# Sign folded into the exponent by a parametric ReLU when float64 gate, value and out weights are converted

## The chip, the cores and the metric

The program runs on 1 core of one Trainium2 chip. The metric is device time in microseconds (us) for one execution. In the names of the trace PE is TensorE (PEld its weight loads), DVE is VectorE, ACT is ScalarE, POOL is GpSimd and SP is SyncE, whose queue (SPq) issues the transfers here.

## The reference

Attention with a local window and block summaries feeds a gated feed-forward layer with an RMS norm, and that feeds a second feed-forward layer with an ELU.

```python
def _moe_ref(x, w_gate, w_val, w_out, rms_g):      # x: 1536 x 512, d_ff 1536
    rms = np.sqrt(np.mean(x * x, axis=-1, keepdims=True) + 1e-06)
    xn = x / rms * rms_g
    g = xn @ w_gate
    silu = g * (1.0 / (1.0 + np.exp(-g)))
    val = xn @ w_val
    return (silu * val @ w_out).astype(np.float32)

def _moe2_ref(x, w_in, w_out):                     # d_ff 2048
    h = x @ w_in
    g = np.where(h > 0.0, h, np.exp(np.minimum(h, 0.0)) - 1.0)
    return (g @ w_out).astype(np.float32)
```

The attention has 2 batches, 8 heads, 768 positions and a head size of 64. The five weight matrices arrive as float64, so the kernel has to turn them into float32 itself.

## The kernel before

The 1536 tokens are three blocks of 512. Attention runs in 24 tiles of 64 positions (`add_tile`): scores `s`, row maximum `nm`, exponentials `e`, the transposed weights `at`, their copy `ats`, and the product with the values, `pv`, which is copied into `xT`. Block 0 is normed in two halves of 256 tokens (`add_norm`): squares `sq`, their sums by matmul `pss`, the mean on VectorE (`ms`), the inverse root on GpSimd (`y`), diagonals `dg` on VectorE, and the matmul `prs` that spreads them over the partitions, after which `scale_x` scales `xT`. A wide name such as `ss0slice(256, 512, None)` is the second half of `pss0`, `rs0slice(256, 512, None)` the second half of `prs0`.

Each block then goes through 12 chunks of the first layer (`add_block1`: gate `pg`, value `pv_0c` to `pv_11c`, product `th` and `act`, down projection `acc`) and later through 16 chunks of the second (`add_block2`: `ph`, `ex`, `act`, `acc`). Matmul operands are split into a high part (a cast on ScalarE, line 272) and a low part (a subtraction, line 283), and three products of the parts are summed. Chunk 0 of block 0 skips the split and multiplies in plain float32 (`project_f32`, line 836).

A weight tile is 128 x 512 numbers. `fetch` (lines 376 and 379) loads it as float64 into `st_<kind><chunk>`, where the kinds are g, v, o (gate, value, out) and i, p (the second layer). There are four `st` buffers, and `fetch` of a fifth tile waits until one is free. Four steps convert a tile:

- `convert_a` (line 278, ScalarE) scales the high 32-bit words, read as float32, by 2^-112, in place, which moves the exponent to the bias of float32;
- `convert_b` (line 395, VectorE) shifts them left by three bits and masks the sign away, into `raw_<kind><chunk>`;
- `convert_c` (line 400, VectorE) puts the sign bit back;
- `convert_d` (line 406, VectorE) adds the bits that the low words hold, and with it the `st` buffer is free.

The order on every engine and on SyncE's queue comes from a planner, `Order.issue`. Each step is added with an engine or a choice of them, a cost and a due time; the planner runs a list schedule with those costs, takes the ready step with the earliest due time on each engine, and then issues the steps in the order in which they started. Engines work through that order strictly. A table `SHIFT` moves the due times of some steps by stage (the names `convert_b`, `convert_c` and `convert_d` are among its keys). VectorE and GpSimd are taken to share a port, so the planner lets the steps named in `SHARED` run on one of them at a time.

Of the kernel before, what the change touches and what calls it, by code (L numbers as in the profile page):

```python
# [16 lines left out]
AF = mybir.ActivationFunctionType  # L17
ALU = mybir.AluOpType
# [19 lines left out]
class Order:  # L38
# [15 lines left out]
    def add(self, engine, cost, due, fn, *args, r=(), w=(), new=()):  # L54

        due += SHIFT.get((fn.__name__, sum(due >= x for x in EDGES)), 0)
        self.ops.append((engine, cost, due, fn, args, tuple(r), tuple(w), tuple(new)))
# [133 lines left out]
def fused_kernel(ctx: ExitStack, tc: tile.TileContext, q, k, v, w_gate, w_val, w_out, rms_g, w_in2, w_out2, out):  # L191
    nc = tc.nc
# [19 lines left out]
    scale = 1.0 / math.sqrt(D)  # L212
# [3 lines left out]
    add = o.add  # L216
    PE, ACT, DVE, POOL = "PE", "ACT", "DVE", "POOL"
# [8 lines left out]
    def new(tag, name, shape, dtype=F32):  # L226
        T[name] = pools[tag].tile(shape, dtype, tag=tag, name=name)
        return T[name]
# [47 lines left out]
    def times(eng, out, in_, factor):  # L276
        if eng == ACT:
            nc.scalar.mul(out, in_, factor)
        else:
            nc.vector.tensor_scalar_mul(out, in_, factor)  # L280
# [45 lines left out]
    for var in range(3):  # L326
# [11 lines left out]
        out=bb, in_=bb, pattern=[[-half, 8]], compare_op=ALU.is_ge, fill=0.0, base=0, channel_multiplier=1)  # L338
    nc.gpsimd.affine_select(
        out=bb, in_=bb, pattern=[[half, 8]], compare_op=ALU.is_ge, fill=0.0, base=half - 1, channel_multiplier=-1)  # L340
# [14 lines left out]
    for i in range(B * NQ):  # L355
        blk, r = divmod(i, TPB)
# [7 lines left out]
    for c in range(C1):  # L364
        t = chunk1_at[0, c]
        weights += [("g", c, t), ("v", c, t + 2.6), ("o", c, t + 5.2)]
    for c in range(C2):

        t = chunk1_at[NBLK - 1, 0] + 10 + 5.2 * c
# [13 lines left out]
    def words(kind, c):  # L383
        return T[f"st_{kind}{c}"].bitcast(U32).rearrange("p (n w) -> p n w", w=2)[:, :, 1]
# [2 lines left out]

    def convert_a(eng, kind, c):
        hi = words(kind, c).bitcast(F32)
        times(eng, hi, hi, 2.0 ** -112)  # L390

    def convert_b(kind, c):
        hi = words(kind, c)
        t = new("raw", f"raw_{kind}{c}", [P, 512], U32)
        nc.vector.tensor_scalar(
            t, hi, 3, 0x7FFFFFF8, op0=ALU.logical_shift_left, op1=ALU.bitwise_and)

    def convert_c(kind, c):
        t = T[f"raw_{kind}{c}"]
# [8 lines left out]
    def add_weights(kind, c, need):  # L408
        st, raw = f"st_{kind}{c}", f"raw_{kind}{c}"
        add("SP", 1.46, need - (14 if need > T0 + 20 else LEAD), fetch, kind, c, w=[st], new=[("st", st)])  # L410
        add(ANY_SB, 0, need - 8, convert_a, kind, c, r=[st], w=[st])
        add(DVE, 0.34, need - 7, convert_b, kind, c, r=[st], w=[raw], new=[("raw", raw)])
        add(DVE, 0.6, need - 6.5, convert_c, kind, c, r=[st, raw], w=[raw])
        add(DVE, 0.6, need - 6, convert_d, kind, c, r=[st, raw], w=[raw])

    def split_a(eng, b, kind, c):
# [559 lines left out]
    for i in range(B * NQ):  # L976
        b, t = divmod(i, NQ)
# [3 lines left out]
        blk, r = divmod(i, TPB)  # L981
# [7 lines left out]
    for kind, c, need in weights:  # L989
        add_weights(kind, c, need)  # L990
# [5 lines left out]

LOOK, URGENT = 0.2, 20
A0, A_GAP, LATER = 12.1, 1.275, -1.0  # L1000
PRE_0, PRE, VS0, MEAN = 0, 8, 4.5, 9.0
# [56 lines left out]
```

## Time and profile before

| | |
|---|---|
| median of 3 runs | 654.74 us (654.32 to 657.03) |
| profiled execution: time | 653.92 us |
| profiled execution: span of the instructions | 652.2 us |
| TensorE matmul busy | 639.4 us, 98% |
| VectorE busy | 477.2 us, 73% |
| ScalarE busy | 374.5 us, 57% |
| GpSimd busy | 68.7 us, 11% |

The profiled execution took 653.92 us, of which 652.2 us are the span from its first instruction to its last; the other 1.7 us lie around it. The profiled execution is 0.8 us under the median of the runs shown. A busy TensorE is one with a matmul in its pipeline: matmuls overlap, so one that is recorded with 389 ns can start 227 ns after the one before it.

### The profile page before, as it was taken

How to read it: one execution, taken by the hardware profiler on the slowest of the kernel's cores; microseconds unless marked ns; L12 is line 12 of the kernel's file. 1: busy time of each engine (PE TensorE's matmuls, PEld its weight loads, DVE VectorE, ACT ScalarE, POOL GpSimd, SP SyncE). 2: the span in 40 equal slices, each digit the busy share in tenths (PEclk: the TensorE clock that was granted, in tenths of full speed). 3: DMA queues.
4: the chain of work that ended last, by engine and by line, in shares of the span. 5: the costliest groups of instructions: out<-in, count | busy, mean ns of one | idle time of the engine just before them, and what ended most of it. 6: DMA issues, size and time to landing. Idle time of an engine off the chain costs nothing.

```text
span 652.2 us, 9445 instructions
## 1 busy us (share of the span) xinstructions
PE 639.4 (98%) x3440; PEld 528.4 (81%) x3440; DVE 477.2 (73%) x860; ACT 374.5 (57%) x829; POOL 68.7 (11%) x125
## 2 busy tenths in 40 slices
PE   7899999999999999999999999999999999999997
PEld 5788787888888888888888888888888888888886
DVE  6899998998945545599999996555675555755554
ACT  5887888878856655655555555443454444544441
POOL 4731103125200100300000000000000000000000
PEclk9999999999999999999999999999999999999999
DMA  9785995653120400003655520000010000100001
GB/s 255 196 236 163 268 282 162 200 168 88 33 47 3 140 1 2 0 13 119 205 180 163 162 65 1 0 1 1 1 65 0 2 0 1 53 13 2 0 1 64
DMA packets 69917, 54.70 MB, mean 84 GB/s; under 512 B 29168, under 2 KB 64176, under 8 KB 69872
## 3 DMA queue, kind: packets, MB, share of 16 engines
q1 hardware_dynamic: 69872, 54.11, 28.8%
q8 instruction: 27, 0.44, 0.3%
q14 instruction: 18, 0.15, 0.1%
HBM read 49.68 MB, written 3.15 MB: 81 GB/s over the span
## 4 chain that ended last, share of the span: by engine, by line
PE 91%; DVE 3%; DMA 2%; ACT 2%; SPq 1%; issue 1%; POOL 0%; ACTq 0%; POOLq 0%
PE acc L893 35%; PE ph L825 20%; PE pg L825 14%; PE s L617 3%; PE pv L667 2%; PE pv_7c L825 1%; PE pv_9c L825 1%; PE pv_11c L825 1%; PE pv_1c L825 1%; DMA va<-vs 1%; PE pv_10c L825 1%; PE pv_6c L825 1%; PE pv_5c L825 1%; PE pv_8c L825 1%; PE pv_2c L825 1%; PE pv_3c L825 1%
## 5 line engine op out<-in xcount | busy, mean ns | idle before, releaser
L825 PE MATMUL ph<-xb,ws_i 128*128 128x512 f32 x576 | 137.9, 389 | 0.0
L893 PE MATMUL acc<-ws_p,act 128*128 128x512 f32 x576 | 137.7, 389 | 0.0
L825 PEld LDWEIGHTS ph<-xb,ws_i 128*128 128x128 f32 x576 | 108.1, 188 | 22.5
L893 PEld LDWEIGHTS acc<-ws_p,act 128*128 128x128 f32 x576 | 108.1, 188 | 22.4
L893 PE MATMUL acc<-act,ws_o 128*128 128x512 f32 x432 | 106.4, 393 | 0.0
L825 PE MATMUL pg<-x,ws_g 128*128 128x512 f32 (+1 forms) x432 | 106.3, 390 | 0.0
L893 PEld LDWEIGHTS acc<-act,ws_o 128*128 128x128 f32 x432 | 80.2, 188 | 16.6
L825 PEld LDWEIGHTS pg<-x,ws_g 128*128 128x128 f32 x432 | 78.2, 188 | 15.3 <-issue 0.2
L283 DVE TENSOR_TENSOR ws_p<-raw_p,ws_p 128x512 fp32r<-128x512 f32 x48 | 33.1, 690 | 48.8 <-ACT ws_p L272 48.8
L272 ACT CAST ws_p<-raw_p 128x512 fp32r<-128x512 f32 x48 | 29.8, 621 | 63.1 <-PE ph L825 57.3
L272 ACT CAST act<-ex 128x512 fp32r<-128x512 f32 x48 | 29.8, 622 | 55.9 <-DVE ex L873 39.3
L880 DVE TENSOR_TENSOR act<-ex,act 128x512 fp32r<-128x512 f32 x48 | 33.1, 691 | 31.3 <-ACT act L272 30.9
L283 DVE TENSOR_TENSOR ws_i<-raw_i,ws_i 128x512 fp32r<-128x512 f32 x48 | 33.1, 689 | 19.1 <-ACT ws_i L272 19.0
L272 ACT CAST ws_i<-raw_i 128x512 fp32r<-128x512 f32 x48 | 29.7, 619 | 28.5 <-PE ph L825 23.1
L283 DVE TENSOR_TENSOR ws_g<-raw_g,ws_g 128x512 fp32r<-128x512 f32 x35 | 25.6, 732 | 18.4 <-ACT ws_g L272 18.0
L272 ACT CAST ws_o<-raw_o 128x512 fp32r<-128x512 f32 x36 | 22.4, 621 | 26.3 <-PE acc L893 6.3
L272 ACT CAST ws_g<-raw_g 128x512 fp32r<-128x512 f32 x35 | 21.6, 618 | 24.9 <-PE pg L825 13.2
L873 DVE SCALAR_TENSOR_TENSOR ex<-ph,ex 128x512 f32<-128x512 f32 x48 | 33.2, 691 | 1.5
L272 ACT CAST ws_v<-raw_v 128x512 fp32r<-128x512 f32 x35 | 21.7, 619 | 16.7 <-PE pv_1c L825 3.2
L283 DVE TENSOR_TENSOR ws_v<-raw_v,ws_v 128x512 fp32r<-128x512 f32 x35 | 25.0, 714 | 6.0 <-ACT ws_v L272 5.9
L272 ACT CAST act<-th 128x512 fp32r<-128x512 f32 x36 | 22.3, 618 | 11.6 <-PE acc L893 5.8
L865 ACT ACTIVATE ex<-ph 128x512 f32<-128x512 f32 x48 | 28.5, 593 | 0.0
(209 smaller groups left out, 987.6 us busy)
## 6 DMA issues: line engine op xcount, KB each, us to landing
st_i<-in_moe_w_in SPq DMA_DIRECT2D x16, 512.0 KB
st_p<-in_moe_w_out SPq DMA_DIRECT2D x16, 512.0 KB
st_g<-in_moe_w_gate SPq DMA_DIRECT2D x12, 512.0 KB
st_v<-in_moe_w_val SPq DMA_DIRECT2D x12, 512.0 KB
st_o<-in_moe_w_out SPq DMA_DIRECT2D x12, 512.0 KB
va<-in_v SPq DMA_DIRECT2D x20, 192.0 KB
kr<-in_k SPq DMA_DIRECT2D x12, 256.0 KB
vtok<-in_v SPq DMA_DIRECT2D x6, 512.0 KB
```

The costliest lines, as they stand in the source:

```text
L272: nc.scalar.copy(out=out, in_=in_)
L283: (nc.gpsimd if eng == POOL else nc.vector).tensor_sub(out, a, b)
L617: nc.tensor.matmul(pq[:, pr, :], qb[:, t % 2, pr].rearrange("p h c -> p (h c)"), ka[:, pr, :], start=not pre, stop=not pre or pr == NP - 1)
L667: nc.tensor.matmul(pv[64 * h:64 * h + 64, pr, :], va[:, 2 * pr + h, :], at[:, pr, QT * h:QT * h + QT], start=True, stop=True)
L825: nc.tensor.matmul(pt[:, i], wt[:, a, kk * P:(kk + 1) * P], xt[:, c, kk, i], start=(kk == 0 and n == 0), stop=(kk == KM - 1 and n == 2))
L865: nc.scalar.activation(out=new("t2", f"ex{b}_{c}", [P, TB]), in_=T[f"ph{b}_{c}"], func=AF.Exp)
L873: nc.vector.scalar_tensor_tensor(ex, T[f"ph{b}_{c}"], 0.0, ex, op0=ALU.max, op1=ALU.add)
L880: nc.vector.tensor_sub(t[:, 1], T[src], t[:, 0].bitcast(F32))
L893: nc.tensor.matmul(acc, lhsT, rhs, start=(first and n == 0), stop=(last and n == 2))
```

## The change

For the kinds g, v and o the scaling on ScalarE becomes a parametric ReLU with the same scale and a slope of -2^32 for negative numbers. A negative word becomes positive with an exponent that is larger by 32, and 32 in the exponent field is bit 28, which the shift by three bits moves to bit 31, the sign. So `convert_b` needs no mask for these kinds, and `convert_c` is left out: 36 tiles lose one VectorE step. The kinds i and p stay as they were. The planner's input is otherwise the same, and it sets a new order with it.

```diff
     def convert_a(eng, kind, c):
         hi = words(kind, c).bitcast(F32)
-        times(eng, hi, hi, 2.0 ** -112)
+        if kind in SIGNED:
+            nc.scalar.activation(out=hi, in_=hi, func=AF.Prelu, scale=2.0 ** -112, alpha=-2.0 ** 32)
+        else:
+            times(eng, hi, hi, 2.0 ** -112)
 
     def convert_b(kind, c):
         hi = words(kind, c)
         t = new("raw", f"raw_{kind}{c}", [P, 512], U32)
-        nc.vector.tensor_scalar(
-            t, hi, 3, 0x7FFFFFF8, op0=ALU.logical_shift_left, op1=ALU.bitwise_and)
+        if kind in SIGNED:
+            nc.vector.tensor_scalar(t, hi, 3, None, op0=ALU.logical_shift_left)
+        else:
+            nc.vector.tensor_scalar(
+                t, hi, 3, 0x7FFFFFF8, op0=ALU.logical_shift_left, op1=ALU.bitwise_and)
...
         add(DVE, 0.34, need - 7, convert_b, kind, c, r=[st], w=[raw], new=[("raw", raw)])
-        add(DVE, 0.6, need - 6.5, convert_c, kind, c, r=[st, raw], w=[raw])
+        if kind not in SIGNED:
+            add(DVE, 0.6, need - 6.5, convert_c, kind, c, r=[st, raw], w=[raw])
         add(DVE, 0.6, need - 6, convert_d, kind, c, r=[st, raw], w=[raw])
...
+SIGNED = 'gvo'
```

The new order differs from the old one at three places that matter below. The line numbers of the changed kernel are larger by 7 from the attention's steps on.

The first place is TensorE around the norm of block 0's second half, before:

```order
L667 MATMUL pv_7_797<-ats_7_765,va_7_686 64x64 x8
L836 MATMUL pg_0_817<-xT_411,raw_g_547 128x256 x4
L732 MATMUL ss0slice(256, 512, None)_834<-ones, 1)slice(256, 512, None)_824 128x128 x2
L732 MATMUL ss0slice(256, 512, None)_834<-ones, 3)slice(256, 512, None)_827 128x128 x2
...
L836 MATMUL pv_0c<-xT_411,raw_v_633 128x256 x4
L825 MATMUL pg_1_868<-x_807,ws_g_850 128x256 x12
L767 MATMUL rs0slice(256, 512, None)_891<-dg0slice(256, 512, None)_883,ones 128x256
L617 MATMUL s_9_895<-ka_9_667,qbd_133 128x120 x4
L825 MATMUL pv_1c<-x_807,ws_v_886 128x256 x12
```

and in the changed kernel:

```order
L674 MATMUL pv_7_795<-ats_7_762,va_7_679 64x64 x8
L774 MATMUL prs0slice(0, 256, None)_808<-dg0slice(0, 256, None)_792,ones 128x256
L624 MATMUL s_9_813<-ka_9_662,qbd_133 128x120 x4
L739 MATMUL ss0slice(256, 512, None)_835<-ones, 1)slice(256, 512, None)_819 128x128 x2
L739 MATMUL ss0slice(256, 512, None)_835<-ones, 3)slice(256, 512, None)_822 128x128 x2
...
L843 MATMUL pg_0_859<-xT_411,raw_g_547 128x256 x4
L774 MATMUL rs0slice(256, 512, None)_882<-dg0slice(256, 512, None)_874,ones 128x256
L843 MATMUL pv_0c<-xT_411,raw_v_686 128x256 x4
L832 MATMUL pg_1_901<-x_830,ws_g_781 128x256 x12
```

Between the sums of the second half and its spreading there were two half projections (`pv_0c` and `pg_1`); now there is one (`pg_0`). The spreading of the first half and the scores of tile 9 stand ahead of the sums instead.

The second place is VectorE in the same stage, up to the mean of the second half, before:

```order
L773 SCALAR_TENSOR_TENSOR xT_411<-xT_411,g_sb,prs0slice(0, 256, None)_781 128x256 x4
L274 COPY xT_411<-pv_7_797 128x4x64
L622 TENSOR_TENSOR e_8_788<-s_8_787,mask_152 128x480
L810 TENSOR_TENSOR x_807<-xT_411,x_807 128x256 x4
L406 SCALAR_TENSOR_TENSOR raw_g_761<-st_g_628,raw_g_761 128x512
L395 TENSOR_SCALAR raw_v_846<-st_v_709 128x512
L395 TENSOR_SCALAR raw_o_852<-st_o_731 128x512
L400 SCALAR_TENSOR_TENSOR raw_v_846<-st_v_709,raw_v_846 128x512
L737 TENSOR_SCALAR ms0slice(256, 512, None)_860<-ss0slice(256, 512, None)_834 128x2
```

and in the changed kernel:

```order
L629 TENSOR_TENSOR e_8_784<-s_8_783,mask_152 128x480
L633 TENSOR_REDUCE nm_8_811<-e_8_784 128x4
L780 SCALAR_TENSOR_TENSOR xT_411<-xT_411,g_sb,prs0slice(0, 256, None)_808 128x256 x4
L817 TENSOR_TENSOR x_830<-xT_411,x_830 128x256
L274 CAST x_830<-xT_411 128x256
L817 TENSOR_TENSOR x_830<-xT_411,x_830 128x256 x3
L399 TENSOR_SCALAR raw_v_857<-st_v_684 128x512
L744 TENSOR_SCALAR ms0slice(256, 512, None)_864<-ss0slice(256, 512, None)_835 128x2
```

The sign step of `raw_v` is gone from the rows ahead of the mean, and so are two steps of other weights; the mask and row maximum of tile 8 stand ahead of the scaling.

The third place is ScalarE around the cast of `act` of chunk 2, block 0, before:

```order
L278 ACTIVATE st_g_1077<-st_g_1077 128x512
L272 CAST ws_v_1179<-raw_v_1124 128x512
L272 CAST act_0_2_1182<-th_2_1144 128x512
L278 ACTIVATE st_v_1126<-st_v_1126 128x512
L272 COPY ats_9_1202<-at_9_1184 120x512
```

and in the changed kernel:

```order
L391 ACTIVATE st_v_1053<-st_v_1053 128x512
L272 CAST ws_g_1116<-raw_g_1008 128x512
L272 COPY ats_9_1128<-at_9_1111 120x512
...
L391 ACTIVATE st_o_1097<-st_o_1097 128x512
L391 ACTIVATE st_g_1107<-st_g_1107 128x512
L391 ACTIVATE st_v_1120<-st_v_1120 128x512
L272 CAST ws_o_1215<-raw_o_1076 128x512
L391 ACTIVATE st_o_1138<-st_o_1138 128x512
L272 CAST act_0_2_1224<-th_2_1158 128x512
```

Ahead of that cast ScalarE used to scale 13 tiles (the last is gate 4); now it scales 18 (the last is out 5).

## Rows read from the trace of the kernel before

**Rows 1.** Stretches: us; busy (instructions) of PE, PEld, DVE, ACT, POOL; clock; DMA share; GB/s.
```profile
26.00:36.00 10.00, 9.27 (x132) 8.44 (x132) 8.31 (x23) 9.90 (x41) 6.84 (x12) 1.00 0.94 264
36.00:50.00 14.00, 13.29 (x126) 11.88 (x125) 13.44 (x31) 9.83 (x19) 5.79 (x6) 1.00 0.84 227
50.00:170.00 120.00, 119.03 (x759) 97.29 (x759) 111.72 (x206) 97.55 (x242) 30.07 (x37) 1.00 0.65 182
170.00:280.00 110.00, 110.00 (x624) 90.62 (x623) 63.65 (x116) 68.37 (x175) 11.66 (x18) 1.00 0.10 30
```

**Rows 2.** The page's chain that ended last: share of the span by engine.
```profile
PE 91%; DVE 3%; DMA 2%; ACT 2%; SPq 1%; issue 1%; POOL 0%; ACTq 0%; POOLq 0%
```

**Rows 3.** The same chain in order of time: start us, us, what; its sign steps.
```profile
37.91 0.67 DVE raw_o L400
...
39.61 0.57 DVE raw_g L400
...
45.30 0.60 DVE raw_v L400
```

**Rows 4.** Groups by line, a kind's sign steps: shapes, count | busy us, mean ns | idle.
```profile
L400 DVE SCALAR_TENSOR_TENSOR raw_g<-st_g,raw_g 128x512 uint32<-128x512 uint32 x12 | 8.2, 686 | 0.0
```

**Rows 5.** Groups by line: ScalarE's scaling, a tanh, its table load; VectorE's shift, a cast.
```profile
L278 ACT ACTIVATE st_o<-st_o 128x512 f32<-128x512 f32 x12 | 8.3, 690 | 0.5 <-DMA st_o<-in_moe_w_out 0.5
L854 ACT ACTIVATE th<-pg 128x512 f32<-128x512 f32 x36 | 21.3, 592 | 4.7 <-PE pg L825 4.3 <-POOL slice(0, 512, None)_2119 L725 0.2
L272 ACT ACT_TABLE_LOAD x1 | 1.3, 1283 | 0.8 <-PEq L1044 0.8
L395 DVE TENSOR_SCALAR raw_g<-st_g 128x512 uint32<-128x512 uint32 x12 | 6.0, 504 | 0.2 <-ACT st_g L278 0.2
L274 DVE CAST xb<-x 128x512 fp32r<-128x512 f32 x4 | 1.7, 423 | 2.0 <-PE ph L825 2.0
```

**Rows 6.** TensorE in order of time, 40 to 50 us: start, us, what, idle before.
```profile
40.60 0.69 PE L667 MATMUL pv<-ats,va 120*64 120x64 f32 x16
41.22 1.99 PE L836 MATMUL pg<-xT,raw_g 128*128 128x256 f32 x8
43.05 0.61 PE L732 MATMUL lice(256, 512, None)_834<-ones,lice(256, 512, None)_824 128*128 128x128 f32 x4
...
44.83 1.89 PE L836 MATMUL pv_0c<-xT,raw_v 128*128 128x256 f32 x8
46.37 1.77 PE L825 MATMUL pg<-x,ws_g 128*128 128x256 f32 x12
48.42 0.67 PE L767 MATMUL lice(256, 512, None)_891<-lice(256, 512, None)_883,ones 128*128 128x256 f32 x2 [0.27 <-DVE lice(256, 512, None)_883 L753]
48.93 1.05 PE L617 MATMUL s<-ka,qbd 128*128 128x120 f32 x8
49.74 0.48 PE L825 MATMUL pv_1c<-x,ws_v 128*128 128x256 f32 x2
```

**Rows 7.** VectorE in order of time: the mean of the second half.
```profile
45.82 0.14 DVE L737 TENSOR_SCALAR lice(256, 512, None)_860<-lice(256, 512, None)_834 128x2 f32<-128x2 f32 x1
```

**Rows 8.** SyncE's queue and TensorE in order of time: the values of tile 9, issued and used.
```profile
47.73 0.76 SPq L580 DMA_DIRECT2D va<-vs  x1
...
74.70 0.51 PE L667 MATMUL pv<-ats,va 120*64 120x64 f32 x10
```

**Rows 9.** TensorE's waits from 50 to 280 us: us in total, times, longest.
```profile
PE kt L454 <- ACT ats L272: 0.8, 1, 0.8
PE pv L667 <- ACT ats L272: 0.2, 1, 0.2
```

**Rows 10.** Busy time by stretch as in rows 1: transfers in three stretches.
```profile
50.00:60.00 10.00, 10.00 (x66) 9.02 (x66) 10.00 (x23) 8.16 (x22) 2.62 (x5) 1.00 0.53 151
60.00:70.00 10.00, 10.00 (x63) 8.13 (x62) 9.70 (x21) 8.87 (x30) 1.36 (x1) 1.00 0.60 171
80.00:90.00 10.00, 9.80 (x74) 7.74 (x74) 9.59 (x17) 7.33 (x19) 1.30 (x1) 1.00 1.05 308
```

## The prediction

> **What bounds the kernel now.** I read the busy time by stretch first, then the chain that ended last, then TensorE in order of time in the one stage where it still waits, then its waits after that.
>
> TensorE bounds nearly everything. It is on the chain for 91% of the span [rows 2], and its clock is granted in full in every stretch shown [rows 1]. The reader should look at what it leaves idle. From 170 to 280 us nothing is left: 110.00 of 110 us are busy. From 50 to 170 us it is idle for 0.97 us of 120, though VectorE is busy for 111.72 us there. From 26 to 50 us it is idle for 0.73 + 0.71 = 1.44 us [rows 1]. Matmuls overlap in the pipeline, so short gaps hide inside a busy time, but this is the order of what can be won: 2.4 us, wherever VectorE's help comes. The change does nothing before 26 us, since TensorE's order up to there is the same and no sign step stands there on the chain, and it leaves TensorE's order alone after about 170 us.
>
> A difference of 0.5%, 3.3 us here, is about what a measurement of this kernel can tell from no change.
>
> **What is removed.** 36 sign steps go; one kind's twelve take 686 ns each [rows 4], and the other two kinds run the same instruction on the same shape: 36 x 0.686 = 24.7 us less for VectorE, nearly all of it between 26 and 170 us, where VectorE is busy for 8.31 + 13.44 + 111.72 = 133.5 of 144 us [rows 1]. This is cover work. TensorE runs on while VectorE is full, and only three sign steps stand on the chain, 0.67 + 0.57 + 0.60 = 1.84 us, all three in the norm of block 0 [rows 3]. If the order stayed as it is, those 1.84 us would be the gain.
>
> **What is exchanged.** ScalarE's scaling takes 690 ns for an out tile [rows 5]. No row shows a parametric ReLU. From below I take the tanh of the same size, 592 ns, from above twice the scaling, 1380 ns; the nearest row is the scaling itself, same tile, same strided words, one pass, so I take 690 ns and a difference of nothing. At the upper end ScalarE would get 36 x 0.69 = 24.8 us more; it is idle for 0.10 + 4.17 + 22.45 = 26.7 us between 26 and 170 us [rows 1], so even that fits in sum, though not everywhere in time. The Trainium skill (ScalarE: Activation LUTs, section What ACT_TABLE_LOAD costs) says that each per-partition pointer operand adds about 93 ns to an ACTIVATE; were the slope passed in that way, 36 of them would be an estimated 3.3 us more of ScalarE work by that page, inside the same idle time, and the sum would stay as it is. The shift without a mask is still one VectorE pass over the same words: the gate tiles' shift takes 504 ns, a cast of the same size, with no arithmetic on it, 423 ns [rows 5]. I take no difference, since the pass over the words is the same; the bounds are nothing and 36 x 0.08 = 2.9 us less work under cover.
>
> **What is moved.** The planner sets a new order, and one place costs. Before, TensorE had `pv_0c` and `pg_1` (starts 44.83 and 46.37, 1.54 us from start to start, and 1.77 us by its record less an overlap of some 0.3 us, so about 1.5 us) between the sums of the second half and its spreading at 48.42, and so it idled for only 0.27 us [rows 6] while VectorE took the mean at 45.82 [rows 7], GpSimd the root, and VectorE made the diagonals. From the mean to the spreading that is 2.60 us of latency. In the new order only half of `pg_0` stands there, 43.05 - 41.22 = 1.83 us by its start and the next one's [rows 6], and the scores of tile 9 (48.93 to 49.74, 0.81 us) have been done earlier.
>
> When do the sums run in the new order? They wait for the squares of tile 7, whose `pv` starts at 40.60 [rows 6]. I leave that start where it is: in both orders the scores of tile 8 ahead of it wait for the same transposed queries and their copies on ScalarE. Then the sums run from 43.05 to about 44.9 as before. If VectorE is free at once, the spreading starts 2.6 us and a hop later, at 47.6. If VectorE is late, I walk it: from the end of tile 8's scores at about 40.6 it has the mask, the row maximum, four half-wide scalings, four half-wide parts of `x`, and a half-wide cast with a shift ahead of the mean, in width seven passes of 0.69 us [rows 4] or 4.8 us, so the mean stands at 45.4 with hops to 45.6 and the spreading at 48.2. I take the middle, 47.9, that is 0.5 us earlier than before. But behind it TensorE still has to do 1.54 + 1.5 - 0.81 = 2.2 us more than before. So this place costs 2.2 - 0.5 = **1.7 us**. The bounds: 2.3 us if the spreading is no earlier, and 0.35 us if the two sign steps that went from the rows ahead of tile 7's work (0.67 [rows 3] and 0.69 [rows 4], one out and one value step) pull everything forward by their full 1.36 us.
>
> Two queues are passed as well. On SyncE's, loads of weights move ahead of the values `va` of tiles 9 to 11; those of tile 9 were issued at 47.73 and used at 74.70 [rows 8], a lead that hides several loads, so I take nothing. On GpSimd's, the key copies of tiles 10 and 11 move ahead of the second half's root; they wait for scores that are over before the sums, so I take nothing there either, and the upper bound of the 1.7 us covers it.
>
> After 50 us TensorE waits twice, 0.8 and 0.2 us, both for ScalarE's copy of `ats` [rows 9]. The new order puts other work around those copies and a shorter VectorE queue ahead of them. Of the 0.97 us I take half away, **-0.5 us**; the bounds are -0.97 us and nothing, and what new waits could add is a rival below.
>
> **The sum.** 653.92 + 1.7 - 0.5 = 655.1 us for an execution like the profiled one. That one is 0.8 us under the median of the runs shown; against the median it is 654.7 + 1.2 = **655.9 us**. The bounds of the two terms give 654.1 to 657.1.
>
> **Rivals.**
>
> *The cover is not missed* (faster). The three sign steps leave the chain, 1.84 us, the two waits after 50 us go, 0.97 us, and TensorE's reordering costs nothing because the front of the norm moves forward by as much. For it: all three steps stood in one stage, on the chain [rows 3]. Against it: the latency of 2.60 us from mean to spreading is none of theirs and now has less work over it. It gives 654.7 - 2.8 = 651.9 us.
>
> *ScalarE waits for weights that have not landed* (slower). The place is the cast of `act` of chunk 2: five more tiles are scaled ahead of it, and ScalarE works strictly in order, so the cast, the down projection behind it and TensorE stand behind the last of those landings. Five tiles of 512 KB are 2.6 MB, at the 308 GB/s of the busiest stretch [rows 10] 1.7 us each and 8.5 us together. From 50 to 70 us 151 and 171 GB/s moved [rows 10], so (308 - 161) x 20 us = 2.9 MB fit in, just. It decides against the change when the transfers start over one tile's time, 1.7 us, late, for they wait for an `st` buffer each. If it happens in two chunks, TensorE loses 2 x 1.7 = 3.4 us on top of the forecast: 659.3 us. For it: transfers already fill 80 to 90 us. Against it: ScalarE waited 0.5 us in all for the out tiles [rows 5].
>
> *The new function needs another table* (slower). ScalarE loads its table once now, 1283 ns [rows 5]. If the parametric ReLU were not in that table, each of 36 scalings would have a load ahead of it and one behind: 72 x 1.283 = 92 us, against 26.7 us of idle time, so some 66 us of it late: 720 us. The Trainium skill (ScalarE activation tables: per-element evaluation and per-set limits, section What a function is on this engine) states that rule: functions of different sets are one load apart, those of one set need no switch. Against it stands that ScalarE's order in the changed kernel has a single table load too, at its start.
>
> **Chances.** The forecast 0.63: it follows from TensorE's order, which is known. The cover not missed 0.18, the late weights 0.17, the table 0.02. The range from 652.0 to 659.4 leaves out half of the first rival, half of the second and the third, 0.19. Faster by over 0.5% (under 651.5) is the lower part of the first rival, 0.07. Slower by over 0.5% (over 658.0) is nearly all of the second, the third and a tail of the forecast, 0.19. The rest, 0.74, is within 0.5%.
>
> **What would show it.** Right: VectorE's busy time falls by about 24 us to some 453 us, and the `st` scalings keep about 0.69 us; TensorE has an idle time of 1 to 2 us ahead of the spreading of the second half, released by VectorE's diagonals, and the first `acc` starts 1 to 2 us later than before; after 170 us the traces agree, shifted. Wrong: the spreading starts 2 us or more earlier than 48.42 (then the first rival), ScalarE's waits for `st` landings sum to several us and TensorE waits after 50 us for `act` (the second), more than one table load (the third). A parametric ReLU of over 1 us with ScalarE full from 50 to 170 us would undo the price that I took.

## The result and the profile after

The changed kernel takes 659.89 us (median of 5 runs, 659.34 to 660.12) beside 654.87 us for the kernel before on the same chip: a ratio of 1.007 (95% interval 1.0052 to 1.0087), **slower by 0.7%**. The forecast was 655.9 us, its range ended at 659.4, and "slower" had 0.19. The profiled execution has a span of 658.0 us, 5.8 us more than before.

The stretches of the changed kernel, columns as in [rows 1]:

```profile
26.00:36.00 10.00, 9.11 (x142) 8.13 (x141) 9.28 (x25) 9.75 (x41) 7.41 (x13) 1.00 0.91 252
36.00:50.00 14.00, 11.95 (x106) 10.55 (x105) 12.84 (x30) 10.48 (x27) 5.81 (x9) 1.00 0.76 215
50.00:170.00 120.00, 115.77 (x743) 94.61 (x744) 92.89 (x171) 92.36 (x227) 29.63 (x34) 1.00 0.66 183
170.00:280.00 110.00, 110.00 (x635) 90.72 (x630) 62.11 (x107) 67.80 (x174) 10.83 (x18) 1.00 0.11 31
```

VectorE did get its relief: 92.89 us busy of 120 instead of 111.72. Yet TensorE idles more: 2.05 us from 36 to 50 (0.71 before) and 4.23 us from 50 to 170 (0.97 before). From 170 us on it has no gap, as before. So 1.34 + 3.26 = 4.6 us of the 5.8 are new gaps of TensorE in these two stretches; the rest is 0.3 us of gaps elsewhere and 0.9 us that TensorE is busy longer (640.3 beside 639.4). The page's chain, on which TensorE had 91% before [rows 2], and the groups of the steps that changed:

```profile
PE 85%; DVE 5%; ACT 4%; DMA 3%; SPq 2%; issue 1%; ACTq 0%; DVEq 0%
```

```profile
L391 ACT ACTIVATE st_o<-st_o 128x512 f32<-128x512 f32 x12 | 8.3, 690 | 0.6 <-DMA st_o<-in_moe_w_out 0.6
L391 ACT ACTIVATE st_v<-st_v 128x512 f32<-128x512 f32 x12 | 8.2, 686 | 4.8 <-DMA st_v<-in_moe_w_val 4.7
L272 ACT ACT_TABLE_LOAD x1 | 1.3, 1283 | 0.8 <-PEq L1052 0.8
L399 DVE TENSOR_SCALAR raw_g<-st_g 128x512 uint32<-128x512 uint32 x12 | 5.9, 490 | 2.8 <-ACT st_g L391 2.8
```

The instructions cost what they cost before: 690 ns for the parametric ReLU beside 690 ns for the scaling [rows 5], one table load, 490 ns for the shift beside 504. What is new is behind the bar: ScalarE waits 4.7 us for landings of value tiles. TensorE's waits from 36 to 280 us (us in total, times, longest), of which [rows 9] had two, 0.8 and 0.2 us, after 50 us:

```profile
PE slice(0, 512, None)_2203 L774 <- DVE dg1slice(0, 512, None)l L768: 1.2, 1, 1.2
PE qt L446 <- ACT kT L272: 1.2, 1, 1.2
PE lice(256, 512, None)_835 L739 <- ACT st_v L391: 1.0, 1, 1.0
...
PE acc L900 <- DVE act L887: 0.8, 2, 0.6
PE acc L900 <- ACT act L272: 0.6, 1, 0.6
```

Three places after 65 us stand out. TensorE waits at 105 us for the last copies of block 1's transposed keys (`qt`), at 117 to 118 us for `act` of chunk 5, and at 166 us for the diagonals of block 1's spreading (`slice_2203`). Measured from matmul start to matmul start, less the usual distance, they are 1.40, 0.72 + 0.84 and 1.42 us: about 4.4 us. The third row is in the front, the norm of block 0.

### The profile page after: what moved, and what is told of

Read it like the earlier page. It is cut to its first block, busy times and chain, and to the rows that moved or that the text cites. A ratio compares the mean times of both kernels' runs of the same rounds, so it can differ in the third digit from the quotient of the medians.

```text
span 658.0 us, 9401 instructions
## 1 busy us (share of the span) xinstructions
PE 640.3 (97%) x3440; PEld 529.0 (80%) x3440; DVE 461.4 (70%) x831; ACT 370.7 (56%) x822; POOL 68.6 (10%) x125
## 4 chain that ended last, share of the span: by engine, by line
PE 85%; DVE 5%; ACT 4%; DMA 3%; SPq 2%; issue 1%; ACTq 0%; DVEq 0%
PE acc L900 34%; PE ph L832 20%; PE pg L832 13%; DMA st_v<-in_moe_w_val 2%; PE s L624 2%; PE pv L674 2%; PE pv_2c L832 1%; PE pv_9c L832 1%; PE pv_11c L832 1%; PE pv_7c L832 1%; PE pv_3c L832 1%; PE pv_8c L832 1%; PE at L663 1%; DMA qq<-in_q 1%; ACT e L640 1%; PE pv_10c L832 1%
## 5 line engine op out<-in xcount | busy, mean ns | idle before, releaser
L900 PE MATMUL acc<-act,ws_o 128*128 128x512 f32 x432 | 108.0, 395 | 1.4 <-DVE act L887 0.8
L640 ACT ACTIVATE e<-e,nm 128x120 f32<-128x120 f32 x64 | 24.5, 385 | 9.4 <-DVE nm L633 9.4
L887 DVE TENSOR_TENSOR act<-th,act 128x512 fp32r<-128x512 f32 x36 | 25.4, 705 | 5.5 <-ACT act L272 4.9
```

Of the source, the lines that this page charges most:

```text
L640: nc.scalar.activation(out=e[:, pr, :], in_=s[:, pr, :], func=AF.Exp, bias=nm[:, pr:pr + 1], accum_out=ss[:, pr:pr + 1])
L887: nc.vector.tensor_sub(t[:, 1], T[src], t[:, 0].bitcast(F32))
L900: nc.tensor.matmul(acc, lhsT, rhs, start=(first and n == 0), stop=(last and n == 2))
```

## The experiments

The planner's list of operations was fixed, either as the changed kernel has it (the **new order**) or as before with the sign steps left out (the **old order**), and single operations were moved in it. Ratios are to the kernel before on the same chip, with 95% intervals.

### Is it the instructions or their order?

**The old order with the new steps.** The planner still counts the sign step, and nothing is issued for it.

```diff
-        if kind not in SIGNED:
-            add(DVE, 0.6, need - 6.5, convert_c, kind, c, r=[st, raw], w=[raw])
+        add(DVE, 0.6, need - 6.5, convert_c, kind, c, r=[st, raw], w=[raw])
...
     def convert_c(kind, c):
+        if kind in SIGNED:
+            return
```

> The order of the kernel before, instruction for instruction on every engine, with the change's instructions in it: the parametric ReLU and the shift without a mask for gate, value and out tiles, and nothing where their sign step stood. Theory A, the new order costs, the new instructions do not: no slower than the kernel before, 653.0 to 654.9 us, VectorE about 24 us less busy, waits after 50 us as in [rows 9]. Theory B, the parametric ReLU costs (a longer or blocking step on ScalarE): 657 us or more, with ScalarE's scalings over 0.69 us or idle gaps behind them.

Measured: 653.67 us, ratio 0.9977 (0.9966 to 0.9989), faster than both kernels. From 50 to 170 us TensorE idles 0.74 us, and one wait is left:

```profile
50.00:170.00 120.00, 119.26 (x764) 97.80 (x762) 92.44 (x175) 97.67 (x242) 28.89 (x37) 1.00 0.64 181
```

```profile
PE kt L462 <- ACT ats L272: 0.7, 1, 0.7
```

So the new instructions by themselves gain 0.2%; the loss comes with the order.

**The new order with the old steps**: the three old instructions, in the new order, each sign step issued right ahead of the step that follows it.

```diff
     def convert_d(kind, c):
+        if kind in SIGNED:
+            convert_c(kind, c)
```

> The order of the changed kernel on every engine, with the conversion of the kernel before: scaling without the ReLU, shift with mask, and the sign step put back directly ahead of the step that adds the low bits. Theory A (order): as slow as the changed kernel or slower, 659.5 to 663 us, since VectorE has 24.7 us more to do in the same order. Theory B (the new instruction): back to about 655 us.

Measured: 674.48 us, ratio 1.0298 (1.0284 to 1.0311). That is slower, as theory A has it, but far above its 663 us. The sign steps cost 14.6 us in the new order (a part of it is clock, as the last section shows); in the old one they cost 1.3. The relief of VectorE is real, but it is the new order that needs it.

**Which part of the order?** The two orders were joined at the first down projection (58 us): old up to there and new behind it, and the reverse.

> New instructions; the steps are issued in the order of the kernel before up to the first down projection (about 58 us), and from there in the order of the changed kernel. Theory A with its two places: the norm of block 0 costs nothing, what comes after 58 us costs the 3.5 us that the traces show there: 656.5 to 658.5 us. Rival A2, a single late front from which all the rest follows: 653 to 655 us.

> New instructions; the order of the changed kernel up to the first down projection, then that of the kernel before. Theory A with its two places: the norm of block 0 costs its 1.2 to 1.7 us and the rest nothing or half a microsecond less than nothing: 655.5 to 656.6 us. Rival A2: 658.5 to 660 us.

Measured: 660.12 us, ratio 1.008 (1.0063 to 1.0097), for the old front with the new rest, and 655.56 us, ratio 1.0013 (1.0004 to 1.0023), for the new front with the old rest. With the old rest, the new front costs 655.56 - 653.67 = 1.9 us (2.4 by the ratios). With the new front, the new rest costs 659.89 - 655.56 = 4.3 us (3.7 by the ratios). With the new rest, the old front gains nothing: its trace has a new wait of 1.1 us of the first down projection for a gate step of VectorE at 61 us. Where the first projection `pv_0c` starts its second half, TensorE is still 1.2 us ahead of the changed kernel (53.85 beside 55.06), and at the product at 64 us it is 0.4 us behind (63.92 beside 63.54). The first expectation was missed for that reason.

### One wait mended at a time

Each run changes one place of the new order.

```diff
 PE   turn_k (1, 2, 1)
+ACT  copy_k (1, 2, 1, 0)
+ACT  copy_k (1, 2, 1, 1)
...
 ACT  convert_a (v, 7)
 ACT  copy_v (1)
-ACT  copy_k (1, 2, 1, 0)
 ACT  convert_a (o, 7)
-ACT  copy_k (1, 2, 1, 1)
```

> One edit in the new order: on ScalarE the two copies of the transposed keys of tile 2 of block 1 stand right behind the transposes, ahead of the scaling of v7, the copy of the block's mean values and the scaling of o7; the other four engines keep their order. In the changed kernel TensorE waits 1.2 us (105.1 to 106.5) for the second of them. Theory (each new wait comes from where an operation stands in an in-order queue, and its price reaches the end): the wait goes and the time falls by 1.0 to 1.4 us, to 658.5 to 658.9. Rival (the wait is only where a general lateness shows, and the next wait takes over what is won): the wait goes or shrinks, TensorE waits as much within the next 20 us, and the time stays within 0.4 us of 659.9. Rival of the landing weights: the two copies were not late by the scalings' place but by landings ahead of them; then the wait stays at about 1.2 us.

Measured: 664.51 us, ratio 1.014 (1.0124 to 1.0156), 4.6 us slower than the changed kernel, outside all that was expected. The wait for the keys shrank from 1.2 to 0.3 us, and another grew; then TensorE's clock fell. Its waits (first row), and stretches of it as in [rows 1]:

```profile
PE acc L925 <- ACT act L296: 2.7, 1, 2.7
```

```profile
118.00:121.00 3.00, 0.33 (x4) 0.15 (x2) 1.60 (x5) 3.00 (x12) 0.90 (x3) 1.00 1.13 291
121.00:123.00 2.00, 1.62 (x6) 1.10 (x7) 2.00 (x6) 2.00 (x7) 0.00 (x0) 0.97 1.16 317
123.00:125.00 2.00, 2.00 (x8) 1.64 (x7) 2.00 (x4) 1.93 (x5) 0.00 (x0) 0.50 0.11 35
125.00:127.00 2.00, 2.00 (x20) 1.33 (x19) 2.00 (x6) 1.36 (x8) 0.00 (x0) 0.68 0.26 70
```

TensorE was busy for 0.33 of 3 us, ran on, and then had half of its clock (0.50) for 2 us and part of the next 2. Of the 4.3 us between the two profiled spans, these places explain 1.9 us more at `act`, 0.3 us less at the keys (the product ahead of `qt` now waits too), and 2 x 0.03 + 2 x 0.50 + 2 x 0.32 = 1.7 us of clock: 3.3 us. Some 1.5 us more lie ahead of 61 us, where the edit changes nothing, and stay open; 0.6 us of shorter waits go the other way.

```diff
-PE   spread (1)
 PE   project (pg0_11, second half)
 PE   project (pv0_11c, first half)
+PE   spread (1)
 PE   apply_v (1, 4)
```

> One edit in the new order: on TensorE the spreading of the root of block 1 stands behind two more groups that are ready (the second half of pg_11 and the first half of pv_11c); with it only the product of tile 4 of block 1 moves. In the changed kernel TensorE waits 1.2 us (166 to 167.9) there for VectorE's diagonals. Theory: two half groups of about 0.85 us cover the wait; it goes, and the time falls by 0.8 to 1.4 us, to 658.5 to 659.1; less if the scaled x of block 1 is then late for its first gate product. Rival (the wait is handed on): VectorE makes the scaled x later by as much, TensorE waits for that in its next stage, and the time stays within 0.4 us of 659.9.

Measured: ratio 1.0072 (1.0059 to 1.0084), no change. The wait at 166 us is gone and another of 1.3 us stands at 175 us. VectorE in order of time (start, us), and the matmul that waits:

```profile
169.29 2.73 DVE L805 SCALAR_TENSOR_TENSOR xT<-xT,g_sb,slice(0, 512, None)_2224 128x512 f32<-128x512 f32 x4 [1.71 <-PE slice(0, 512, None)_2224 L799]
171.93 0.68 DVE L890 SCALAR_TENSOR_TENSOR th<-th,pg 128x512 f32<-128x512 f32 x1
...
175.87 0.69 DVE L912 TENSOR_TENSOR act<-th,act 128x512 fp32r<-128x512 f32 x1
...
176.61 1.40 PE L925 MATMUL acc<-act,ws_o 128*128 128x512 f32 x5 [1.25 <-DVE act L912]
```

The scaled `x` now starts at 169.29, and the gate of chunk 11 stands behind it in VectorE's line, though its input `th` was there at 168.6. The wait was handed on.

```diff
-    pool("st", 4, True)
+    pool("st", 6, True)
```

(for the buffers alone; the planner's list stays that of four)

> One edit in the new order: the weights land in six buffers in place of four, every engine's order as in the changed kernel. ScalarE waits 6.5 us between 50 and 170 us for landings there, 2.3 us of it for v8, and TensorE's two waits for act of chunk 5 (1.4 us, 117.2 to 118.8) stand behind that. Theory (my second rival in its general form: transfers start late since they wait for a buffer): ScalarE's landing waits fall under 2 us, TensorE's wait for that act goes, and the time falls by 1.0 to 1.8 us, to 658.1 to 658.9. Rival (the transfers are as slow as the memory lets them be, or the buffer is not what holds them): landing waits stay over 4 us and the time stays within 0.4 us of 659.9.

Measured: 658.88 us, ratio 1.0052 (1.004 to 1.0064). By the ratios this gains 1.2 us; the intervals overlap, but the traces agree: TensorE's waits for that `act` shrink from 1.4 to 0.2 us, and ScalarE's landing waits from 6.5 to 1.4.

```diff
+PE   project_f32 (pv0_0c, first half)
+PE   project (pg0_1, first half)
 PE   spread (0, second half)
-PE   project_f32 (pv0_0c, first half)
...
-PE   project (pg0_1, first half)
```

> One edit in the new order: on TensorE the first halves of pv_0c and of pg_1 stand ahead of the spreading of the second half of block 0's norm again, as in the order before; all else as in the changed kernel. Theory (that the place costs what it cost by itself, 655.56 - 653.67 = 1.9 us): the wait ahead of the spreading falls from about 2 us to under 0.7, the first down projection starts 1.2 to 1.9 us earlier, and the time falls by as much, to 658.0 to 658.7. Rival (what is won in the front is given back in the new rest, as the run with the old front and the new rest suggests with 660.12): the first down projection starts earlier by 1.2 to 1.9 us, but by 125 us the gain is gone, and the time is 659.5 to 660.3.

Measured: ratio 1.0082 (1.0067 to 1.0097), no gain. Both expectations had the first down projection earlier; in the profile it starts at 62.67 us, 3.0 us later than in the changed kernel (59.66). TensorE now waits 1.5 us at 54.5 us, in the same front, for VectorE's split of `v1`:

```profile
PE pv_1c L857 <- DVE ws_v L307: 1.5, 1, 1.5
```

### Mended together

The first run has six buffers and the keys ahead; the second adds the spreading two groups later, with VectorE's gate of chunk 11 ahead of the scaled `x` and its `act` ahead of the casts; the third adds the filled front with the split of `v1` ahead of the scaled `x`.

> Two edits in the new order: six landing buffers, and on ScalarE the two key copies ahead of the scalings. Alone, the key copies made it slower, 1.014 of the kernel before, since the scalings behind them freed their buffers later and g8 and v8 landed late (a 2.7 us wait of TensorE for act at 118 us and then half the granted clock for some microseconds). Theory (the feed of the weights is what hands the key wait on): with six buffers the landing waits do not come back, the 1.2 us wait for the keys is won, and the time is 0.9 to 1.5 us under the run with six buffers alone (ratio 1.0052), a ratio of 1.003 to 1.004. Rival (ScalarE is simply behind, and whatever goes first makes the next late): act of chunk 5 is late again by 1 us or more and the ratio is 1.005 or above.

> As the run before it, and the spreading of block 1 two groups later, this time with the gate and act of chunk 11 ahead of the scaled x and its casts on VectorE and ScalarE, since the run with the spreading alone moved showed TensorE's wait handed on to that act (1.5 us at 174.9). Theory (the 4.3 us that the new order costs behind the front is these three waits, 1.4 + 1.5 + 1.4): the wait at 166 goes with none in its place, and the ratio is 1.001 to 1.002, that of the run with the new front and the old rest (1.0013). Rival (the waits are handed on again): TensorE waits over 1 us between 165 and 185 us, and the ratio stays at or above that of the run before it.

> As the run before it, and the first halves of pv_0c and pg_1 ahead of the spreading of block 0's second half, this time with VectorE's split of v1 ahead of the scaled x, since the run with the front alone filled showed the wait handed on to that split (1.55 us at 54.5). Theory (front and rest are both order, and all of it can be won back inside the new order): 1.0 to 2.0 us less than the run before it, a ratio of 0.998 to 1.000, as in the old order with the new steps (0.9977). Rival (the front's gain is handed on to the casts or the first act, as with the old front and the new rest): under 0.5 us less.

Measured: ratios 1.0115 (1.0098 to 1.0132), 1.009 (1.0074 to 1.0106) and 1.0136 (1.0114 to 1.0158), all three above what the theories expected. Six buffers don't keep `g8` from landing late once the keys go ahead: ScalarE waits 2.8 to 3.9 us for it, TensorE 2.1 to 3.2 us for `act`, and the granted clock is 0.87, 0.87 and 0.77 from 117 to 130 us. Once the gate goes with it, the spreading's mend gains 1.6 us (1.0115 to 1.009; the intervals overlap, but the trace has no wait there any more). Why the third run is slower than the second was not settled: its profile, taken of the longest of its five executions (667.0 us), shows a granted clock of 0.78 from 36 to 50 us, behind idle time that lies ahead of the edit.

The same kind of edit in the old order, one half group ahead of the one wait that is left there:

```diff
+PE   project (pv0_5c, first half)
 PE   turn_k (1, 2, 0)
 PE   turn_k (1, 2, 1)
...
-PE   project (pv0_5c, first half)
```

> The order before with the new steps (ratio 0.9977), and one edit: on TensorE the first half of pv_5c stands ahead of the transposes of the keys that wait 0.74 us for ScalarE's copy of ats at 98 us. Theory (a wait that ready work can cover, with VectorE now less than full behind it): 0.5 to 0.9 us less, a ratio of 0.9963 to 0.997, which would be the fastest version of this study. Rival (handed on to the next key copies or the first down projection): within 0.3 us of 0.9977.

Measured: ratio 0.9981 (0.9972 to 0.999), no gain over 0.9977: the wait moved from the keys to the scores at 105 us, which wait 0.8 us for GpSimd's key copy.

### What holds the loads

Both runs with the keys ahead had `g8` late, with four buffers and with six, so the buffer was not what held it. SyncE's line in the changed kernel (start, us, what), ScalarE's copy `vm`, the scaling that waits for `v8` and the cast of `act` of chunk 5 behind it, SyncE's longest wait from 95 to 118 us, and one stretch:

```profile
96.89 0.84 SPq L584 DMA_DIRECT2D va<-in_v  x1
104.48 3.05 SPq L556 DMA_DIRECT2D vs<-vm  x4
107.64 0.46 SPq L379 DMA_DIRECT2D st_g<-in_moe_w_gate  x1
108.20 0.44 SPq L379 DMA_DIRECT2D st_v<-in_moe_w_val  x1
```

```profile
104.20 0.26 ACT L552 COPY vm<-vp 128x128 f32<-128x128 f32 x1
...
114.46 0.68 ACT L391 ACTIVATE st_v<-st_v 128x512 f32<-128x512 f32 x1 [2.32 <-DMA st_v<-in_moe_w_val]
...
117.05 0.63 ACT L272 CAST act<-th 128x512 fp32r<-128x512 f32 x1
```

```profile
SPq L556 <- ACT kT L272: 7.4, 1, 7.4
```

```profile
99.00:107.00 8.00, 6.67 (x90) 5.14 (x89) 6.00 (x11) 7.83 (x15) 1.82 (x3) 1.00 0.25 68
```

SyncE stands at the transfer of block 1's value means, which needs ScalarE's copy `vm`, from 96.89 + 0.84 = 97.73 to 104.48 us, 6.75 us, and needs 3.05 us to issue its four parts; `g8` and `v8` are next in its line. Meanwhile 68 GB/s move. The row of the wait names `kT` as what ended it and counts 7.4 us, up to the end of that copy (105.14 us), when the first part is already being issued; the transfer starts within 0.02 us of the end of `vm`, its input. The keys' edit had moved `vm` from 104.20 to 107.27 us, 1.5 us of that with a later start, and so `g8` with it.

The late loads cost TensorE time through ScalarE's order. In the kernel before, `g8` was issued later still, at 110.61 us, and TensorE did not wait: there ScalarE cast `act` of chunk 5 (first row) ahead of the scalings of `g8` (second row) and `v8` (120.28 us):

```profile
112.42 0.62 ACT L272 CAST act<-th 128x512 fp32r<-128x512 f32 x1
...
118.16 0.69 ACT L278 ACTIVATE st_g<-st_g 128x512 f32<-128x512 f32 x1
```

In the new order both scalings stand ahead of that cast, which runs at 117.05 us though VectorE had its input `th` ready at 114.30. Moving the cast ahead of them was not tried.

```diff
+ACT  copy_v (1)
 ACT  convert_a (g, 7)
 ACT  convert_a (v, 7)
-ACT  copy_v (1)
```

> One edit in the new order, with four buffers as in the changed kernel: on ScalarE the copy vm of block 1's value means stands ahead of the scalings of g7 and v7. Theory (SyncE's line: the transfer of vm waits for that copy, and the loads of g8 and v8 stand behind it): the copy is 1.1 us earlier, so are the issues of vs<-vm, g8 and v8; TensorE's wait for act of chunk 5 falls from 1.5 us to 0.4 to 0.9, and the ratio is 1.0055 to 1.0065 against the 1.007 of the changed kernel (0.6 to 1.0 us). Rival (the landing buffers hold them, which the scalings put back by 0.26 us): landing waits as before or longer, ratio 1.007 or above.

Measured, with four buffers: ratio 1.0052 (1.0033 to 1.0072), 1.2 us less than the changed kernel, with intervals that overlap; TensorE's waits for that `act` fall to 0.2 us. In its trace TensorE is 1.2 us later than in the changed kernel at 94 us (94.08 beside 92.92) and 0.4 us earlier at 120 us (119.68 beside 120.06). So the loads, issued at 107.76 and 108.34 us, are no earlier by the clock, but 1.1 us earlier against TensorE.

```diff
+SP   fetch (g, 8)
+SP   fetch (v, 8)
 SP   place_v (1)
-SP   fetch (g, 8)
-SP   fetch (v, 8)
```

> Six landing buffers and one edit on SyncE: the loads of g8 and v8 stand ahead of the transfer vs<-vm that waits for ScalarE. Theory (SyncE's line): both loads are issued near 98 us in place of 107 to 108, the memory is busy where it was idle (99 to 107 us), ScalarE's landing waits between 110 and 117 us go, TensorE has no wait for act of chunk 5, and the ratio is 1.004 to 1.005 (with six buffers alone 1.0052). Rival (bandwidth): the landings of g8 and v8 are no earlier, or others become late, and the ratio is that of six buffers alone or above.

Measured, with six buffers: ratio 1.005 (1.0032 to 1.0067). SyncE issues both loads 13 us earlier, and ScalarE has no landing wait left between 50 and 170 us:

```profile
94.47 0.51 SPq L404 DMA_DIRECT2D st_g<-in_moe_w_gate  x1
95.08 1.38 SPq L404 DMA_DIRECT2D st_v<-in_moe_w_val  x1
104.21 3.06 SPq L582 DMA_DIRECT2D vs<-vm  x4
```

So SyncE's line held the loads. An earlier `vm` alone is worth 1.2 us by the ratios, with four buffers; with six, TensorE's wait for `act` was 0.2 us already, so taking the loads out of the line adds nothing to 1.0052 but leaves the landings free of `vm`, which the next two runs need. The line is not all of it: with six buffers alone it was as before (`v8` issued at 108.76 us), and the scaling of `v8` started 5.2 us after that issue, with the earlier `vm` 5.0 us, in the changed kernel 6.3 us. Why it landed sooner stays open.

> As the run before it, and on ScalarE the copy vm and then the two key copies of tile 2 ahead of the scalings of g7, v7 and o7. Theory (the keys' edit lost because it put vm, and so SyncE's line, back): now TensorE's wait at 105 goes and no landing wait takes its place, 1.0 to 1.4 us less than the run before it, a ratio of 1.002 to 1.0035. Rival (handed on whatever the feed): act of chunk 5 is late by over 1 us again, ratio over 1.005.

> As the run before it, and the spreading of block 1 two groups later with the gate and act of chunk 11 ahead of the scaled x and its casts; with the keys' edit as it was then (1.0115), this edit brought the ratio to 1.009. Theory (the 4.3 us behind the front are these three waits and nothing else): no wait of TensorE over 0.6 us between 65 and 280 us, and a ratio of 1.000 to 1.002, beside 1.0013 for the new front with the old rest. Rival (a part of the 4.3 us has another source): the waits are gone and the ratio is still above 1.003.

Measured: ratios 1.005 (1.0033 to 1.0067) and 1.0023 (1.0006 to 1.0039). With `vm` and the keys ahead the wait at 105 us is gone, nothing lands late, and still nothing is won: the scores at 110 us wait instead. In the second run, VectorE's sums of the keys, GpSimd's key copies and the scores:

```profile
105.17 0.43 DVE L427 TENSOR_SCALAR raw_g<-st_g 128x512 uint32<-128x512 uint32 x1 [1.58 <-ACT st_g L419]
105.52 0.77 DVE L442 SCALAR_TENSOR_TENSOR raw_o<-st_o,raw_o 128x512 uint16<-128x512 uint16 x1
...
107.49 1.20 DVE L497 TENSOR_REDUCE ksum<-kT 128x32 f32<-128x1024 f32 x1
...
108.77 1.27 POOL L621 TENSOR_SCALAR ka<-ksum 128x96 f32<-128x96 f32 x1 [6.69 <-DVE ksum L497]
...
110.09 1.15 PE L653 MATMUL s<-ka,qbd 128*128 128x120 f32 x8 [1.58 <-POOL ka L621]
```

The sums of the keys stand behind the conversion steps of three tiles that nothing needs yet. The spreading's mend gives 1.8 us (1.005 to 1.0023), and no wait takes its place.

### Closing the account

```diff
+DVE  max_k (1, 2)
 DVE  convert_b (g, 7)
 DVE  convert_b (v, 7)
...
-DVE  max_k (1, 2)
```

> As the run with loads, keys and spreading mended (ratio 1.0023), and on VectorE the sums of the keys of tile 2 stand ahead of the shifts of g7, v7 and o7. Theory (the 4.3 us are these three waits): the scores at 108 to 110 us wait under 0.4 us for GpSimd's key copy in place of 1.6, no wait of TensorE over 0.6 us is left between 65 and 280 us, and the ratio is 0.9995 to 1.0012, at or just under the new front with the old rest (1.0013, which has one wait of 0.9 us itself). Rival (handed on once more, to the shifts that now come later): TensorE waits over 1 us between 108 and 130 us, ratio 1.002 or above.

Measured: 655.46 us (12 runs, 654.59 to 658.83), ratio 1.0024 (1.0009 to 1.0039). By the median that is 4.4 us less than the changed kernel and level with the new front and the old rest (655.56); by the ratios it is 3 us, since four of the twelve runs are 1.9 to 3.4 us above the median. The expected ratio, 0.9995 to 1.0012, was missed, and by the ratios this last edit gains nothing (1.0023 before it). The trace has what the theory asks for, and that the three waits are the whole 4.3 us rests on it and on the median. Of the three waits none is left. TensorE's waits from 36 to 280 us, all of them ahead of 62 us, and its stretch:

```profile
PE lice(256, 512, None)_835 L769 <- ACT st_v L420: 1.0, 1, 1.0
PE s L654 <- ACT qbd L307: 0.8, 1, 0.8
PE lice(256, 512, None)_882 L804 <- DVE lice(256, 512, None)_874 L790: 0.3, 1, 0.3
PE acc L930 <- DVE act L917: 0.2, 1, 0.2
```

```profile
50.00:170.00 120.00, 119.64 (x769) 98.57 (x769) 94.42 (x176) 94.52 (x232) 29.68 (x34) 1.00 0.63 174
```

TensorE idles 0.36 us of 120 instead of 4.23, and the profiled span is 653.6 us, 4.4 us under that of the changed kernel. The last run puts the old front ahead of this, with one gate step of VectorE moved up:

```diff
 DVE  invert (0, 8)
+DVE  gate_c (0, 1)
 DVE  row_max (0, 9)
...
-DVE  gate_c (0, 1)
```

> The order before up to the first down projection and behind it the new order with the mends of the run before it; and on VectorE the gate of chunk 1 that frees a PSUM bank for the first down projection stands ahead of the row maximum and the shifts, since with the old front and the new rest TensorE waited 1.2 us at 61 us for it. Theory (front and rest add up when no wait is handed on): 1.4 to 2.0 us less than the run before it, a ratio of 0.9970 to 0.9985, as the old order with the new steps (0.9977). Rival (the front's gain is lost at that seam in any case): within 0.6 us of the run before it.

Measured: 654.81 us, ratio 1.0004 (0.9994 to 1.0015): 0.7 us less by the median, 1.3 us by the ratios, between the two expectations. Of the front's 1.9 us a part is handed on at the seam once more, a wait of 1.6 us at 62 us:

```profile
PE pv L710 <- ACT ats L307: 1.6, 1, 1.6
```

No version is faster than the old order with the new steps.

## Why the prediction was wrong, step by step

**Removed and exchanged: right where the order stayed.** The parametric ReLU takes 0.69 us, the shift does not change, and one table load is left. The Trainium skill (ScalarE activation tables: per-element evaluation and per-set limits, section What a function is on this engine) says that only functions of different sets need a switch; the single table load agrees. VectorE's busy time fell by 22.2 us with the old order (477.2 to 455.0), near the forecast 24, and by 15.8 with the new one (to 461.4): the new plan gives VectorE other work, such as 6 copies of `ats` in place of 3. The gain forecast for an unchanged order was 1.84 us; measured are 1.3 us by the medians, 1.5 by the ratio.

**The norm of block 0 (+1.7 us): right in size, in part by luck.** The pair of runs gives 1.9 us (2.4 by the ratios), and the first down projection starts 1.72 us later than before:

```profile
57.94 1.40 PE L893 MATMUL acc<-act,ws_o 128*128 128x512 f32 x5
```

```profile
59.66 0.47 PE L900 MATMUL acc<-act,ws_o 128*128 128x512 f32 x1
```

The first row is the kernel before, the second the changed one. Here is TensorE and VectorE in the changed kernel, beside [rows 6, 7]:

```profile
42.19 1.05 PE L624 MATMUL s<-ka,qbd 128*128 128x120 f32 x8
44.20 0.68 PE L739 MATMUL lice(256, 512, None)_835<-ones,lice(256, 512, None)_819 128*128 128x128 f32 x4 [0.96 <-ACT st_v L391]
...
46.05 1.89 PE L843 MATMUL pg<-xT,raw_g 128*128 128x256 f32 x8
48.24 0.67 PE L774 MATMUL lice(256, 512, None)_882<-lice(256, 512, None)_874,ones 128*128 128x256 f32 x2 [0.29 <-DVE lice(256, 512, None)_874 L760]
```

```profile
42.41 1.65 DVE L780 SCALAR_TENSOR_TENSOR xT<-xT,g_sb,0slice(0, 256, None)_808 128x256 f32<-128x256 f32 x4
...
46.26 0.16 DVE L744 TENSOR_SCALAR lice(256, 512, None)_864<-lice(256, 512, None)_835 128x2 f32<-128x2 f32 x1 [0.28 <-PE lice(256, 512, None)_835 L739]
```

I left the sums at 43.05; they run at 44.20. Their squares are no later than before (ScalarE, 42.17 and 42.71 in both traces), and the row names a scaling of weights that is not their input. What fits, and was not tried by itself, is PSUM: two buffers serve the spreading of the first half, the scores of tile 9 and the sums in turn, so the sums need the buffer that VectorE's four scalings of `x` read until 42.41 + 1.65 = 44.06. The spreading then came at 48.24, at the late end of my walk (48.2), and 1.90 us of TensorE's work more than before lie behind it (59.66 - 48.24 less 57.94 - 48.42), where I had 2.2. Two errors offset each other: the sums came 1.15 us later than I had them, and from the mean to the spreading it took 1.98 us (46.26 to 48.24) where I had 2.60. The sign that I named, 1 to 2 us of idle time ahead of the spreading, did not come: 0.96 us stand ahead of the sums and 0.29 us ahead of the spreading.

**"After 50 us ... I take half away, -0.5 us" with the bounds -0.97 us and nothing: this step failed.** It measured **+4.3 us** (the changed kernel less the new front with the old rest; 3.7 by the ratios). Where the order stayed, TensorE's idle time there fell by 0.23 us (0.97 to 0.74), where I had 0.5. I took the new order's rest as the old one with less VectorE work in it, walked one place of it, and left new waits to a rival. The new plan spent the relief on its own: it put conversions of tiles that are needed later ahead of key copies, of sums of the keys and of an `act` that TensorE needs next, and block 1's spreading where its diagonals are not ready yet. Three waits came of it, and with their causes mended 4.4 us came back by the median and by the profiled spans, 3 us by the ratios.

**SyncE's queue ("I take nothing"): wrong.** I looked at the values of tiles 9 to 11 [rows 8], where the lead was long enough; the queue bit at block 1's value means, 57 us later. The Trainium skill (DMA: Bandwidth & Descriptors, section Issuing engines are not separate DMA queues) says that starting transfers on several engines saves only the time to start them, usually small beside the transfer. The trace shows more than that in the line here: SyncE's 6.75 us of waiting and 3.05 us of issuing stood ahead of two loads while 68 GB/s moved, and an earlier head of that line (`vm`) was worth 1.2 us by the ratios.

**The rivals.** "ScalarE waits for weights that have not landed" came closest, with 659.3 us: ScalarE's landing waits rose to 6.5 us, and TensorE did wait for `act`. Its mechanism is the one that came, an `act` behind scalings on ScalarE. But it was chunk 5 and not chunk 2, what held the issue of the loads was SyncE's line and not the `st` buffers, and it made 1.2 to 1.5 of the 4.3 us. "The cover is not missed" holds for the old order alone, and gives 653.67 us there and not 651.9. "Another table" is out.

## What to carry to other kernels

When an edit changes the input of a planner, two things change: the work and the order. Build the new work in the old order first, since that alone tells what the edit is worth; here it was faster by 0.2%, and the re-planned order lost 0.9% on top of it.

A wait is mended at the operation that holds its line, which need not be the engine or the buffer that a row names: walk each in-order queue back, SyncE's too, until you come to an operation that could have run earlier. And price a mended wait only with what is late next: five of the edits here mended a wait, met another one of 0.8 to 2.7 us within 15 us, and won nothing by it.

## What the runs showed that was not expected

One longer wait cost more than its length. With the keys ahead, TensorE was busy for 0.33 of 3 us and then ran at a granted clock of 0.50, that is 1.2 GHz, for 2 us and more, which took another 1.7 us. Waits of 1.2 to 1.5 us, as in the changed kernel, left the granted clock at 1.00. In the new order with the old steps the granted clock is 0.91 from 50 to 70 us and again from 150 to 170 us, so a part of its 14.6 us is clock and not waiting.
